# Decode attention block, forward and backward: the two batches staggered, so that forward heads of batch 1 run beside backward heads of batch 0

## The chip, the cores and the metric

One core of one Trainium2 chip. The metric is the device time of one execution in microseconds (us), the median of several. An execution with a profile takes as long as one without (the profiled execution of the kernel before took 1852.37 us; the others 1848 to 1858).

## The reference, cut to what matters

```python
B, Sq, D = (2, 1, 512);  H, Sk, Dh = (32, 8192, 128);  F = 1376
# forward (all bf16)
mod = silu(c) @ w_mod                       # 6 x 512 modulation values a batch
h   = layernorm(x) * (1 + ca) + sa
q   = h @ wq                                # one query a head
p   = softmax(q @ k_cache^T * Dh**-0.5)     # k_cache, v_cache: (2, 32, 8192, 128)
o   = p @ v_cache
x   = x + ga * (o @ wo)
h   = layernorm(x) * (1 + cb) + sb
x   = x + gb * ((silu(h @ w1) * (h @ w3)) @ w2)
# and the gradients of all inputs for a given grad_out:
# d_v_cache = p (outer) d_o,  d_k_cache = d_s (outer) q: the same 134 MB each as the caches
```

There are 64 heads (2 batches of 32). K and V of a head are 2.1 MB each, and so are its two gradients. In the forward pass a head needs K and V; in the backward pass it needs V again and writes two gradients. Between them lies a serial chain of small steps: output projection, FFN forward, FFN backward, back through the output projection. A batch's chain needs all 32 forward heads of that batch, and a batch's backward heads need that chain. Nothing ties the two batches to each other.

## The kernel before

The program gives each engine a list of instructions, and its author lays down their order by hand. The engines are named as in the profiles: PE (TensorE), DVE (VectorE), ACT (ScalarE), POOL (GpSimd), and SP (SyncE), which issues the loads here. The unit is a *slot*: 8 transposes of 128 x 128 blocks on PE, the copy of the 8 results out of PSUM (the memory that PE writes to), and what else is due. A head is 8 slots. This is the forward loop; the backward loop is built alike.

```python
NBIG = 10                                   # ten buffers of 16 KB a partition, for K, V, results and weights
def hb(i):
    return i % B, i // B                    # head i: the batches alternate
...
def mm_m(i, g):                             # 8 of the 64 blocks of a head: 16 matmuls
    ...
    for j in range(GRP):
        kk = g * GRP + j
        nc.tensor.matmul(m[:, 0:P + 1], V[i][:, kk, :], t[:, kk % QK, 0:P + 1], ...)
        nc.tensor.matmul(m[:, P + 1:P + 2], K[i][:, kk, :], E2[:, i, kk, 0:1], ...)
...
for t in range(NSLOT + MOFF + 1):           # forward: 64 heads x 8 slots
    i, g = divmod(t, NG)
    ...
    kts[(i, g)] = transposes(K[i], g, g in (2, 6))          # 8 transposes; copy by ACT, or by DVE in 2 of 8
    ...                                                     # 8 one-column matmuls with q: the scores
    scale_k(...)                                            # DVE: K times exp(scores), 4 pieces a head
    mm_m(mi, mg)                                            # 16 matmuls for an earlier head
    if mg == NG - 1:
        ...
        load(K, A_k_cache, mi + 4); load(V, A_v_cache, mi + 3)   # when a head is done
# [cut] the serial chain for both batches at once, in plain program order:
#       attn, x1, layernorm, w1, w3, silu, w2, transposes of w2, w1, w3 and wo, their products
for t in range(NSLOT + LAG + 2 * NQ + 4):   # backward: 64 heads x 8 slots
    kts[(n, g)] = transposes(V[order[n]], g, g in (2, 6))
    ...                                     # 8 one-column matmuls; DVE: outer products in 8 pieces a head
    half_store(...)                         # four stores of 1 MB a head, issued by GpSimd (POOL)
    ...                                     # one small "task" a slot: weight gradients and the like
```

Of the kernel before, what the change touches and what calls it, by code (L numbers as in the profile page):

```python
# [9 lines left out]
F32 = mybir.dt.float32  # L10
# [8 lines left out]
def kernel(  # L19
# [48 lines left out]
    NBIG = 10  # L68
# [4 lines left out]
    def hb(i):  # L73
        return i % B, i // B
# [7 lines left out]
    bigp = ctx.enter_context(tc.tile_pool(name="bigp", bufs=NBIG))  # L82
    ktp = ctx.enter_context(tc.tile_pool(name="ktp", bufs=5))
# [6 lines left out]
    def big():  # L90
        return bigp.tile([P, BIG], BF16, name="big", tag="big")

# [15 lines left out]
    E2 = cst.tile([P, NHD, KK, 2], BF16, name="E2")  # L108
# [31 lines left out]
    V = {}  # L140

    def load(store, src, i):
        b, h = hb(i)
        t = big()
        v = t[:, 0:KK * P].rearrange("p (k d) -> p k d", k=KK)
        qd.dma_start(v, src[b, h].rearrange("(p kk) d -> p kk d", p=P))
        store[i] = v
# [10 lines left out]
    load(K, A_k_cache, 0)  # L158
    load_wq(1)
    load(K, A_k_cache, 1)  # L160
    load_wq(2)
    load_wq(3)
    for a in range(2):
        qd.dma_start(wm_v[a][:, :, M1:MD], wm_d[:, 2 * a:2 * a + 2, M1:MD])
    load(V, A_v_cache, 0)
    load(K, A_k_cache, 2)
    load(V, A_v_cache, 1)
    load(K, A_k_cache, 3)
# [114 lines left out]
    evac_n = [0]  # L283

    def evac(dst, src):
        if evac_n[0] % 2 == 0:
            nc.scalar.copy(dst, src)
        else:
            nc.vector.tensor_copy(dst, src)
        evac_n[0] += 1  # L290

    S_ps = {}
    M_ps = {}
    ek = {}
    kts = {}
    M_t = {}
    MOFF = NG + LAG + 5
    NSLOT = NHD * NG

    def pair(ap, n):  # L300
        return ap.rearrange("p k (a b) -> p k a b", b=2)

    def transposes(src, g, dve):
        tp = tps.tile([P, GRP, P], BF16, name="tp", tag="tp")
        for j in range(GRP):
            nc.tensor.transpose(tp[:, j, :], src[:, g * GRP + j, :], identb[:])  # L306
        kt = ktp.tile([P, GRP, P], BF16, name="kt", tag="kt")
        if dve:
            nc.vector.tensor_copy(kt[:], tp[:])  # L309
        else:  # L310
            nc.scalar.copy(kt[:], tp[:])  # L311
        return kt

    def chain_rowmax(i):
        rm = hw.tile([P, 1], BF16, name="rm", tag="rm")
        nc.vector.tensor_reduce(rm[:], S_ps[i][:, 0:KK], AX.X, ALU.max)
        kts[("rm", i)] = rm

    def chain_b(i):
        s = S_ps[i]  # L320
        nc.tensor.matmul(s[:, P:2 * P], kts.pop(("rm", i))[:].to_broadcast((P, P)), nident[:],  # L321
                         start=True, stop=True)
        nm = hw.tile([P, 1], F32, name="nm", tag="nm")
        nc.vector.tensor_reduce(nm[:], s[:, P:2 * P], AX.X, ALU.min)  # L324
        kts[("nm", i)] = nm

    def chain_e(i):
        s = S_ps.pop(i)
        nc.scalar.activation(E2[:, i, :, :], s[:, 0:KK].unsqueeze(2).to_broadcast((P, KK, 2)), ACT.Exp,  # L329
                             bias=kts.pop(("nm", i))[:], scale=SCL, accum_out=rsum[:, i:i + 1])  # L330

    def scale_k(i, q):
        t = ekp.tile([P, QK, 130], BF16, name="ek", tag="ek")
        ks = slice(q * QK, (q + 1) * QK)
        nc.vector.tensor_tensor(pair(t[:, :, 0:P], QK), pair(K[i][:, ks, :], QK),  # L335
                                E2[:, i, ks, :].unsqueeze(2).to_broadcast((P, QK, P // 2, 2)), ALU.mult)
        nc.gpsimd.tensor_copy(t[:, :, P:P + 1], E2[:, i, ks, 0:1])  # L337
        ek[(i, q)] = t

    def mm_m(i, g):  # L340
# [3 lines left out]
        t = ek[(i, g // 2)]  # L344
        for j in range(GRP):
            kk = g * GRP + j
            nc.tensor.matmul(m[:, 0:P + 1], V[i][:, kk, :], t[:, kk % QK, 0:P + 1],  # L347
                             start=(kk == 0), stop=(kk == KK - 1), skip_group_check=True)
            nc.tensor.matmul(m[:, P + 1:P + 2], K[i][:, kk, :], E2[:, i, kk, 0:1],  # L349
                             start=False, stop=(kk == KK - 1), skip_group_check=True)  # L350
        if g == NG - 1:
            K.pop(i)

    def m_evac(i):
        m = M_ps.pop(i)
        nc.scalar.copy(M_all[:, i, :], m[:, 0:P])  # L356
        nc.vector.tensor_copy(OK[:, i, :], m[:, P:P + 2])  # L357

    KEEPV = 2
    extra = {}  # L360

    def at(slot, f):
        extra.setdefault(slot, []).append(f)

    for pc in range(1, NPC):
        at(2 * pc, lambda pc=pc: q_part(pc))
    at(NG, lambda: mod_part(2 * NC, MC))
# [3 lines left out]
    def load_wo():  # L371
        for a in range(2):
            t = big()
            v = t[:, 0:H // 2 * D].rearrange("p (h d) -> p h d", d=D)
            qd.dma_start(v, A_wo.rearrange("(h p) d -> p h d", p=P)[:, a * (H // 2):(a + 1) * (H // 2), :])
            wo_v.append(v)

    wn = {}
    nfull = F // P

    def load_ffn():
        for nm, ap in (("w1", B_w1), ("w3", B_w3)):
            t = big()
            wn[nm] = t[:, 0:NC * F].rearrange("p (k f) -> p k f", k=NC)
            qd.dma_start(wn[nm], ap.rearrange("(k p) f -> p k f", p=P))
        t = big()
        wn["w2"] = t[:, 0:FC * D].rearrange("p (k d) -> p k d", k=FC)
        qd.dma_start(wn["w2"][:, :nfull, :], B_w2[0:nfull * P].rearrange("(k p) d -> p k d", p=P))
        if FL != P:
            qd.dma_start(wn["w2"][:FL, nfull, :], B_w2[nfull * P:F])  # L390

    M_all = None
    Mt = None
    for t in range(NSLOT + MOFF + 1):
        i, g = divmod(t, NG)
        u = t - (NG + LAG + 2)
        if u >= 0 and u % NG == 0 and u // NG < NHD:
            chain_e(u // NG)
        if i < NHD:
            if g == 0:  # L400
                S_ps[i] = stps()
            kts[(i, g)] = transposes(K[i], g, g in (2, 6))
        for f in extra.pop(t, []):
            f()
        s = t - LAG
        if 0 <= s < NSLOT:
            si, sg = divmod(s, NG)
            b, h = hb(si)
            kt = kts.pop((si, sg))
            for j in range(GRP):  # L410
                cc = sg * GRP + j
                nc.tensor.matmul(S_ps[si][:, cc:cc + 1], kt[:, j, :], qT_bf[:, h, b:b + 1],  # L412
                                 start=True, stop=True)
        for off, f in ((0, chain_rowmax), (1, chain_b)):
            u = t - (NG + LAG + off)
            if u >= 0 and u % NG == 0 and u // NG < NHD:
                f(u // NG)
        u = t - (NG + LAG + 3)
        if u >= 0 and u % 2 == 0 and u // NG < NHD:
            scale_k(u // NG, (u % NG) // 2)  # L420
        u = t - MOFF
        if 0 <= u < NSLOT:
            mi, mg = divmod(u, NG)
            mm_m(mi, mg)
            if mg == NG - 1:
                if mi < NHD - KEEPV:
                    V.pop(mi)
                if mi + 4 < NHD:
                    load(K, A_k_cache, mi + 4)
                if mi + 3 < NHD:  # L430
                    load(V, A_v_cache, mi + 3)
                if mi == min(2, NHD - 5):
                    load_wo()
                if mi == NHD - 3:
                    load_ffn()
        if t == NG:
            load(V, A_v_cache, 2)
        u = t - MOFF - 1
        if u >= 0 and u % NG == NG - 1:
            if M_all is None:  # L440
                Mt = big()
                M_all = Mt[:, 0:NHD * P].rearrange("p (i d) -> p i d", d=P)
            m_evac(u // NG)

    woT = [big(), big()]
    woT_v = [t[:, 0:2 * HD].rearrange("p (k m) -> p k m", k=2) for t in woT]

    def tgroup(blocks, dsts):
        tp = tps.tile([P, GRP, P], BF16, name="tp", tag="tp")
        flat = tp[:].rearrange("p a b -> p (a b)")  # L450
        for o, n, src, rows in blocks:
            nc.tensor.transpose(flat[:n, o:o + rows], src, identb[:rows, :rows])
        for dst, (n, o, w, k) in dsts:
            s = flat[:n, o:o + w]
            if k > 1:
                s = s.rearrange("p (k m) -> p k m", k=k)
            evac(dst, s)

    def t_wo(a, h0):
        nh = min(4, H - h0)  # L460
        blocks = []
        for d2 in range(2):
            for hh in range(nh):
                h = h0 + hh
                src = wo_v[h // (H // 2)][:, h % (H // 2), (2 * a + d2) * P:(2 * a + d2 + 1) * P]
                blocks.append(((d2 * nh + hh) * P, P, src, P))
        tgroup(blocks, [(woT_v[a][:, :, h0 * P:(h0 + nh) * P], (P, 0, 2 * nh * P, 2))])

    tot = mtps()
    nc.tensor.matmul(tot[:, 0:NHD], onesf[:], rsum[:], start=True, stop=True)  # L470
    rtot = col("rtot", H)
    rtot_f = rtot[:].rearrange("p h b -> p (h b)")
    nc.vector.tensor_scalar(rtot_f, tot[:, 0:NHD], 0.5, None, ALU.mult)
# [531 lines left out]
```

## Time and profile before

| | |
|---|---|
| median of 5 runs | 1850.72 us (1848.03 to 1858.42) |
| busy share PE, DVE, ACT | 75%, 61%, 52% |
| moved by DMA | 709.57 MB, mean 383 GB/s |

The average shares say little, because three stages follow each other. First the page of the kernel before: busy share of PE, granted TensorE clock, DMA share in tenths (9 is 90% or more) and GB/s in 40 equal slices of 46 us.

```profile
span 1850.6 us, 58876 instructions
PE   5888999999999999978778777675655565566560
...
PEclk9999999999999999968555558577666556656665
DMA  9998999999999999549999999999999999999996
GB/s 391 411 358 323 385 382 392 389 372 378 356 366 369 364 371 365 220 161 357 413 411 416 416 420 421 399 415 420 421 419 418 418 418 418 420 423 423 418 417 282
DMA packets 79784, 709.57 MB, mean 383 GB/s; under 512 B 8160, under 2 KB 13644, under 8 KB 21932
```

Then the busy times cut into the stretches of the argument: stretch, its length, busy us (and instructions) of PE, weight load, DVE, ACT, POOL, the mean granted clock, the DMA share, GB/s. The cut at 461 us is where forward head 38 would start.

```profile
core 0: us, PE busy (x) PEld busy (x) DVE busy (x) ACT busy (x) POOL busy (x), PEclk, DMA share, GB/s
0.00:461.00 461.00, 414.35 (x9757) 408.37 (x9758) 245.07 (x364) 254.46 (x343) 83.44 (x153) 0.99 0.95 378
461.00:765.00 304.00, 282.96 (x6755) 279.13 (x6753) 171.08 (x239) 171.72 (x235) 57.35 (x105) 0.99 0.91 363
765.00:850.00 85.00, 69.89 (x1430) 65.77 (x1427) 46.73 (x107) 43.71 (x63) 7.16 (x10) 0.78 0.44 160
850.00:1800.00 950.00, 615.91 (x8582) 535.73 (x8579) 654.26 (x692) 481.80 (x602) 150.26 (x278) 0.62 1.01 417
1800.00:1850.60 50.60, 3.77 (x80) 3.29 (x78) 15.72 (x17) 3.89 (x4) 5.84 (x11) 0.57 0.70 294
```

And the waits of PE between 200 and 750 us of the kernel before: engine, line, what it waited for, us in total, times, longest.

```profile
PE m_ps L347 <- issue: 9.5, 12, 1.7
PE m_ps L349 <- issue: 7.9, 11, 1.1
PE tp L306 <- issue: 7.9, 10, 1.1
PE s_ps L412 <- issue: 4.5, 7, 0.8
```

Reading them together:

- Forward, to 765 us: PE is busy over 90% of the time at full clock, and it waits for no other engine and for no load: its entries are all "issue" (time in which it waited for nothing that the profile shows), 30 us of 550. DMA stays at 363 to 378 GB/s. So this stage is taken to be PE-bound, at about 11.5 us a head, where the 4.19 MB of a head need 10.0 us at 418 GB/s.
- The chain, 765 to 850 us: neither is full; 160 GB/s.
- Backward, from 850 us: 417 GB/s with a DMA share of 1.01, PE at a clock of 0.62 and still idle a third of the time. This stage is DMA-bound. Loads and stores share this ceiling although two engines issue them; the Trainium skill ("Trainium Kernel Development and Optimization", Key Constraints) says that the queues of SP, ACT and POOL run on the same 16 DMA engines and interleave, which the one share of 1.01 for both agrees with.

A measure used from here on: the *lost DMA time* of a stretch is its length less its bytes divided by 418 GB/s, the rate of the backward stage. The bytes of a kernel over 418 GB/s plus all its lost DMA time is its span. Before: 1697.5 + 153.1 us.

### The profile page before, as it was taken

The page shows a single profiled execution, that of the slowest core. Times are in us where ns is not written, and L with a number is a line of the kernel's source. Part 1 is how long each engine was busy: PE and PEld are TensorE (multiplying, and loading weights), DVE is VectorE, ACT ScalarE, POOL GpSimd, SP SyncE. Part 2 cuts the span into 40 slices and gives each one's busy share as a digit, 9 for nine tenths or more (in the row PEclk, how much of TensorE's full clock was granted, in tenths as well). Part 3 has the DMA queues.
Part 4 walks back from the last instruction along what each step waited for, and adds up shares of the span by engine and source line. Part 5 has one row for each costly group of instructions (what it writes and reads, how often), then busy time and mean ns, then how long its engine had stood idle before and what let it go on. Part 6 is the DMA issues. An engine that isn't in the chain of part 4 may idle for free. (4 is left out here: it accounts for less than half of the span.)

```text
span 1850.6 us, 58876 instructions
## 1 busy us (share of the span) xinstructions
PE 1386.9 (75%) x26588; PEld 1292.3 (70%) x26588; DVE 1132.9 (61%) x1415; ACT 955.6 (52%) x1244; POOL 304.1 (16%) x557
## 2 busy tenths in 40 slices
PE   5888999999999999978778777675655565566560
PEld 5888999999899999876556566474555555555550
DVE  2455656565555555548565647577876667777682
ACT  3545656556555555348546566474444344444440
POOL 0111212122122211102121111111111111111111
PEclk9999999999999999968555558577666556656665
DMA  9998999999999999549999999999999999999996
GB/s 391 411 358 323 385 382 392 389 372 378 356 366 369 364 371 365 220 161 357 413 411 416 416 420 421 399 415 420 421 419 418 418 418 418 420 423 423 418 417 282
DMA packets 79784, 709.57 MB, mean 383 GB/s; under 512 B 8160, under 2 KB 13644, under 8 KB 21932
## 3 DMA queue, kind: packets, MB, share of 16 engines
q1 hardware_dynamic: 38304, 421.57, 56.7%
q0 software_dynamic: 41216, 284.22, 36.9%
q8 instruction: 208, 3.41, 0.7%
q14 instruction: 44, 0.36, 0.1%
q10 hardware_dynamic: 12, 0.01, 0.0%
HBM read 421.57 MB, written 284.20 MB: 381 GB/s over the span
## 5 line engine op out<-in xcount | busy, mean ns | idle before, releaser
L311 ACT COPY kt<-tp 128x1024 bf16<-128x1024 bf16 x768 | 776.2, 1014 | 675.6 <-PE tp L306 665.8
L306 PE MATMUL tp<-identb,big 128*128 128x128 bf16 x8192 | 796.8, 255 | 28.0 <-issue 15.6
L306 PEld LDWEIGHTS <-big 128*128 128x128 bf16 x8192 | 599.9, 114 | 125.3 <-issue 118.0
L347 PE MATMUL m_ps<-ek,big 128*128 128x129 bf16 x4096 | 411.6, 218 | 11.3 <-issue 10.8
L349 PE MATMUL m_ps<-E,big 128*128 128x1 bf16 x4096 | 383.3, 165 | 11.1 <-issue 10.9
L958 PE MATMUL s_ps<-DO_bf,kt 128*128 128x1 bf16 x4096 | 195.7, 169 | 259.2 <-DVE kt L309 258.7
L958 PEld LDWEIGHTS <-kt 128*128 128x128 bf16 x4096 | 191.5, 110 | 278.9 <-DVE kt L309 277.8
L895 DVE TENSOR_TENSOR big<-QD,E 128x2048 bf16<-128x2048 bf16 x256 | 311.7, 1218 | 116.8 <-DMA out_dram<-big 67.9
L895 DVE TENSOR_TENSOR big<-QD,ds 128x2048 bf16<-128x2048 bf16 x256 | 312.0, 1220 | 91.7 <-PE tp L306 60.6
L309 DVE COPY kt<-tp 128x1024 bf16<-128x1024 bf16 x256 | 176.3, 689 | 302.9 <-PE tp L306 260.6
L347 PEld LDWEIGHTS <-big 128*128 128x128 bf16 x4096 | 346.5, 96 | 14.8 <-issue 14.4
L349 PEld LDWEIGHTS <-big 128*128 128x128 bf16 x4096 | 344.0, 96 | 11.5 <-issue 11.1
L335 DVE TENSOR_TENSOR ek<-big,E 128x2048 bf16<-128x2048 bf16 x256 | 306.7, 1219 | 3.0 <-ACT E L329 2.2
L903 POOL DMA_DIRECT2D out_dram<-big x256 | 136.3, 532 | 822.8 <-DVE big L895 356.2
L337 POOL COPY ek<-E 128x16 bf16<-128x16 bf16 x256 | 143.9, 564 | 626.2 <-ACT E L329 274.2
L412 PE MATMUL s_ps<-qT_bf,kt 128*128 128x1 bf16 x4096 | 178.2, 164 | 12.5 <-issue 9.5
L412 PEld LDWEIGHTS <-kt 128*128 128x128 bf16 x4096 | 158.7, 97 | 16.2 <-issue 12.7
L710 ACT CAST stg<-m_ps 128x512 bf16<-128x512 f32 (+2 forms) x123 | 71.9, 593 | 109.2 <-DMA out_dram<-stg 77.0
L709 PE MATMUL m_ps<-big 2*128 2x512 bf16 (+2 forms) x123 | 71.3, 580 | 38.2 <-ACT stg L710 38.1
L324 DVE TENSOR_REDUCE nm<-s_ps 128x1 f32<-128x128 f32 x64 | 18.7, 292 | 57.9 <-PE s_ps L321 57.9
L357 DVE COPY OK<-m_ps 128x2 f32<-128x2 f32 x64 | 10.2, 159 | 59.2 <-ACT big L356 59.2
L890 ACT CAST QD<-m_ps 128x256 bf16<-128x256 f32 x64 | 24.7, 386 | 11.1 <-PE m_ps L887 11.1
(198 smaller groups left out, 483.8 us busy)
## 6 DMA issues: line engine op xcount, KB each, us to landing
out_dram<-big POOLq DMA_DIRECT2D x256, 1024.0 KB, 28.8
big<-in_A_v_cache_dram SPq DMA_DIRECT2D x126, 2048.0 KB, 13.7
big<-in_A_k_cache_dram SPq DMA_DIRECT2D x64, 2048.0 KB, 9.8
out_dram<-stg POOLq DMA_DIRECT2D x22, 512.0 KB, 19.8
big<-in_A_wq_dram SPq DMA_DIRECT2D x8, 512.0 KB, 14.4
big<-in_A_wo_dram SPq DMA_DIRECT2D x2, 2048.0 KB, 17.3
big<-in_A_wq_dram SPq DMA_DIRECT2D x2, 2048.0 KB, 15.3
big<-in_w_mod_dram SPq DMA_DIRECT2D x2, 1536.0 KB
```

What stands on the lines that cost most here:

```text
L306: nc.tensor.transpose(tp[:, j, :], src[:, g * GRP + j, :], identb[:])
L309: nc.vector.tensor_copy(kt[:], tp[:])
L311: nc.scalar.copy(kt[:], tp[:])
L335: nc.vector.tensor_tensor(pair(t[:, :, 0:P], QK), pair(K[i][:, ks, :], QK), E2[:, i, ks, :].unsqueeze(2).to_broadcast((P, QK, P // 2, 2)), ...
L337: nc.gpsimd.tensor_copy(t[:, :, P:P + 1], E2[:, i, ks, 0:1])
L347: nc.tensor.matmul(m[:, 0:P + 1], V[i][:, kk, :], t[:, kk % QK, 0:P + 1], start=(kk == 0), stop=(kk == KK - 1), skip_group_check=True)
L349: nc.tensor.matmul(m[:, P + 1:P + 2], K[i][:, kk, :], E2[:, i, kk, 0:1], start=False, stop=(kk == KK - 1), skip_group_check=True)
L412: nc.tensor.matmul(S_ps[si][:, cc:cc + 1], kt[:, j, :], qT_bf[:, h, b:b + 1], start=True, stop=True)
L710: nc.scalar.copy(st["t"][:lw, o:o + rw], ps[:lw, 0:rw])
L895: nc.vector.tensor_tensor(pair(dst[:, ks, :], QK), QD[n][:, which, :].rearrange("p (a b) -> p a b", b=2).unsqueeze(1).to_broadcast((P, QK, ...
L903: sq_.dma_start(dst_dram[b, h].rearrange("(p kk) d -> p kk d", p=P)[:, ks, :], t[:, ks, :])
L958: nc.tensor.matmul(DP[sn][:, cc:cc + 1], kt[:, j, :], DO_bf[:, h, b:b + 1], start=True, stop=True)
```

## The change

Intent: put the PE-bound forward work beside the DMA-bound backward work. The heads are ordered batch by batch. All forward heads of batch 0 run; the chain of batch 0 ("chain 0") is cut into 57 small steps, laid two to a slot between the forward slots of batch 1's first heads; then forward heads of batch 1 and backward heads of batch 0 alternate ("pairs"); the chain of batch 1 ("chain 1") is laid under the last backward heads of batch 0; then come batch 1's backward heads with the weight gradients, as before.

It costs something. The chain's transposes of w1, w3 and wo are done once for each batch; the products with w2's transpose become dot products on DVE. The FFN weights are dropped after chain 0 and loaded again for chain 1. V tiles are no longer kept over the turn from forward to backward. The buffers are 5 big ones and 11 of half the size, and a load takes whichever kind is free.

```diff
-    NBIG = 10
+    NBIG = 5
+    NHALF = 11
...
     def hb(i):
-        return i % B, i // B
+        return i // H, i % H
...
+    sA = [NG * i for i in range(H)]                 # start slots of the forward heads
+    CS0 = end_a(sA[H - 1]) + 1                      # chain 0 starts
+    TC = CS0 + (length(ch[0]) + 1) // 2 + 1         # and ends
...
+    while len(sA) < NHD:
+        if s >= TC and len(sC) < H and (not sC or sC[-1] < s - NG):
+            sC.append(s)                            # a backward head of batch 0
+        else:
+            sA.append(s)                            # a forward head of batch 1
+        s += NG
...
+    CS1 = end_a(sA[NHD - 1]) + 1
+    lay(dh[1], lay(dh[0], FS0) + 1)                 # the dot products with w2
+    lay_half(ch[0], CS0)
+    t1 = lay_half(ch[1], CS1)
+    s = max(s, t1 + 4)
+    sC += [s + NG * n for n in range(H)]            # backward heads of batch 1
...
+    for a in range(2):
+        want(FS0 - 3 + a, "big", lambda a=a: load_ffn(a))
+        want(CS0 - 3 + a, "big", lambda a=a: load_wo(a))
+        want(CS1 + a, "big", lambda a=a: load_ffn(a))      # the second load of the FFN weights
...
+    at(TC, PL_TASK, ffn_done)                       # drops the FFN weights
+    at(sC[0] - 6, PL_FREE, start_keep)              # from here 2 half buffers are kept for results
```

(The comments are added here. Cut: the bookkeeping of slots and loads, the chain rewritten as steps, the forward and backward parts under new names.) By these rules 38 forward heads come before the first pair, there are 26 pairs, and chain 1 lies under six backward heads.

## The prediction

> **What bounds it now.** Three stages, read from the engine-busy table cut into stretches.
> (1) Forward, 0 to about 765 us. PE is busy 96% of 200-400 us at clock 1.00, and waits there for nothing but its own issue (list of waits). The exp of heads 0 and 35 start at 41.1 and 443.9 us: 11.5 us a head. The loads need only 4.19 MB a head, 10.0 us at 418 GB/s, and DMA runs at 370-384 GB/s. PE-bound.
> (2) The serial chain (output projection, FFN forward and backward), about 765-850: DMA falls to 3 GB/s at 780-800; some 57 us of DMA time are lost.
> (3) Backward, 850 to the end: 414-421 GB/s, DMA share 1.01: DMA-bound, 6.3 MB and about 15 us a head; PE clock 0.61-0.70.
> 709.6 MB at 418 GB/s would take 1697 us; the other 153 us are forward 79, chain 57, end 15.
>
> **What the change does.** Batch by batch: 38 forward heads, the chain of batch 0 laid between the forward slots of heads 32-37, then 26 pairs of one forward head of batch 1 and one backward head of batch 0, then the chain of batch 1 under six backward heads, then 32 backward heads with the weight gradients. PE-bound forward work is set beside DMA-bound backward work; about half of the big buffers become half-size.
>
> **Costed.**
> - Bytes: no V tiles kept over the turn (+4.2 MB), FFN weights twice (+4.2 MB): 718 MB, 1717 us at 418 GB/s (+20).
> - Forward-only stage: head 38 would start at about 461 us by the measured 1.44 us a slot. Chain 0 now sits on the bounding engine: about 28 groups of 8 transposes and 8 matmuls, 0.66 us each from the trace's spacings (56 and 26 ns), plus some 260 one-column matmuls: 25 us, with waits about 40; dot products on DVE about 5. So the pairs start at about 505 us, with about 181 MB loaded (433 us of DMA): 73 us lost.
> - Pairs: 10.5 MB, 25.1 us of DMA. PE needs 11.5 + 5.3 = 16.8 us at full clock, DVE about 17.6, ACT about 14: DMA should bind. The doubt is the clock. The Trainium skill ("TensorE: Matmul & The Clock Gate", Part 1) says that the array runs at half clock until a window of about 3.4 us was busy, and falls back after an idle one; this trace agrees: at 1300-1358 us it alternates between 0.50 and 1.00, going cold after idle gaps of about 5 us. All at half clock, a pair would need about 30 us. I expect oscillation, 0.3 us a pair lost: 8 us.
> - Chain 1 is hidden under backward heads: 0-5 us. End: about 15 us, as now.
> Sum: 1717 + 73 + 8 + 15 = about 1812 us. The 57 us gap goes and 26 forward heads stop being PE-bound; chain 0's PE time and 20 us of bytes are paid.
>
> Predicted: **1812 us**, 80% range 1775 to 1850. Faster by over 2%: 0.52; within 2%: 0.43; slower by over 2%: 0.05.
>
> **What would show each step.** No slice of the DMA row near zero in the middle; first backward-V transposes at 490-520 us; before that 345-375 GB/s; after it at least 405 nearly to the end; PE clock 0.7 to 1.0 in the pairs; 717-719 MB; forward slots of heads 32-37 about 2.3 us.
>
> **What would make it wrong.** Slower: PE cold in the pairs, so that a pair takes 27-30 us (+50 to +120); PE waiting for K or V because a load sits behind a store for its half buffer; GpSimd's in-order queue holding forward copies behind store issues; chain 0 waiting 1-2 us at each of its 57 steps. Faster: chain 0 hides between forward slots, or more is prefetched.

(Read again from the trace: the idle gaps of PE at 1300 to 1358 us that go before half clock are 6.2 to 7.4 us long, not about 5, and the clock falls 2.5 to 3.1 us after they begin.)

## The result, and the profile after

The changed kernel took 1828.36 us (median of 9; 1825.49 to 1834.32), the kernel before 1852.03 us on the same chip (median of 16). The ratio is 0.9871, 95% interval 0.9852 to 0.989: 1.3% faster, within the 2% that count as the same.

The page of the changed kernel, the same rows:

```profile
span 1824.9 us, 60769 instructions
PE   6888999999887777777878777757976867768363
...
PEclk9999999997987888788787778858655555767665
DMA  9998999996599999999999999989999999999997
GB/s 384 422 413 336 383 396 391 378 364 239 202 404 404 419 422 422 416 412 423 419 422 418 424 416 415 415 350 370 419 406 410 411 424 419 418 422 399 425 399 308
DMA packets 98993, 718.11 MB, mean 394 GB/s; under 512 B 10112, under 2 KB 16972, under 8 KB 26284
```

The dip at 765 to 850 us is gone from the middle. But there is a new one in slices 10 and 11 (about 410 to 500 us, 239 and 202 GB/s) and a shallow one in slices 27 and 28 (350 and 370). The stretches of the changed kernel are forward heads 0-31; chain 0; pairs; chain 1; the rest of the backward heads; the end:

```profile
core 0: us, PE busy (x) PEld busy (x) DVE busy (x) ACT busy (x) POOL busy (x), PEclk, DMA share, GB/s
0.00:410.00 410.00, 366.58 (x8638) 359.97 (x8639) 231.88 (x375) 227.21 (x308) 101.94 (x168) 1.00 0.97 385
410.00:520.00 110.00, 97.51 (x2203) 94.92 (x2201) 72.07 (x165) 42.21 (x59) 15.87 (x31) 0.89 0.66 247
520.00:1150.00 630.00, 490.65 (x9689) 474.68 (x9688) 423.16 (x500) 324.24 (x450) 107.80 (x225) 0.81 1.01 418
1150.00:1270.00 120.00, 79.61 (x1647) 74.97 (x1645) 71.72 (x139) 67.26 (x90) 14.60 (x25) 0.77 0.93 373
1270.00:1750.00 480.00, 344.48 (x4448) 272.76 (x4446) 304.21 (x340) 288.89 (x443) 82.44 (x150) 0.60 1.01 415
1750.00:1824.90 74.90, 35.09 (x598) 33.04 (x596) 58.35 (x61) 29.32 (x40) 12.22 (x23) 0.64 0.84 342
```

Worked out from finer slices of the same view, at 418 GB/s:

| lost DMA time, us | before | after |
|---|---|---|
| first forward heads | 43.7 (to 461 us, heads 0-37) | 32.4 (to 410 us, heads 0-31) |
| chain 0, with forward heads 32-37 | in the chain below | 45.0 |
| the other 26 forward heads | 40.2 | 0.0 (the pairs) |
| chain of both / chain 1 | 52.4 | 12.9 |
| backward | 1.7 | 3.4 |
| end | 15.1 | 13.2 |
| sum | 153.1 | 106.9 |
| bytes / 418 GB/s | 1697.5 (709.57 MB) | 1718.0 (718.11 MB) |
| span | 1850.6 | 1824.9 |

So 40 us came from the forward heads that are now in pairs, and 40 from the chain (52.4 less 12.9). Against them stand 34 us for chain 0, which now lies in the PE-bound stage (32.4 + 45.0 against 43.7), and 20 us for 8.5 MB more. What is left is 26 us.

Chain 0 can be timed by the exp instruction of the forward heads, one a head. In the kernel before, heads 32 and 37:

```profile
410.50 0.37 ACT L329 ACTIVATE E<-s_ps,nm 128x128 bf16<-128x128 f32 x1
...
466.05 0.37 ACT L329 ACTIVATE E<-s_ps,nm 128x128 bf16<-128x128 f32 x1
```

In the changed kernel, heads 32 and 37:

```profile
408.63 0.37 ACT L425 ACTIVATE e<-s_ps,nm 128x128 bf16<-128x128 f32 x1
...
506.46 0.37 ACT L425 ACTIVATE e<-s_ps,nm 128x128 bf16<-128x128 f32 x1
```

The columns are start, duration, engine, line, operation. Both kernels reach head 32 within 2 us of each other. The next five heads take 55.6 us before and 97.8 us with chain 0 between their slots: 42 us more. In the pairs the 25 exps from 533.0 to 1135.6 us are 25.1 us apart, the DMA time of 10.5 MB. There PE is at a clock of 0.81 and idle 22% of the time: it no longer binds.

Where the 42 us go can be read from PE's instructions between these two exps, each given the time until the next one starts, less idle time. The chain's own instructions take 28.7 us. The forward slots' instructions take 59.6 us instead of 52.9, which goes with a clock at half for 23.9 us. PE is idle for 9.6 us instead of 2.7; in the list of waits 7.3 us of this are waits for DVE. That is 28.7 + 6.7 + 6.9 us.

The longest waits of PE in chain 1 of the changed kernel, 1150 to 1270 us (L740 is the first product with w1 or w3; L387 the transposes of K and V):

```profile
PE s_ps L740 <- DMA big<-in_B_w_dram: 11.8, 1, 11.8
PE tp L387 <- DMA big<-in_A_v_cache_dram: 6.7, 2, 5.9
PE s_ps L678 <- DVE O_bf L670: 5.2, 1, 5.2
```

### The profile page after: what moved, and what is told of

It reads as the page before. It is cut to its first block, busy times and chain, and to the rows that moved or that the text cites. A ratio compares the mean times of both kernels' runs of the same rounds, so it can differ in the third digit from the quotient of the medians. Undisturbed runs are those within 1.5% of the kernel's fastest.

```text
span 1824.9 us, 60769 instructions
## 1 busy us (share of the span) xinstructions
PE 1413.9 (77%) x27206; PEld 1310.3 (72%) x27206; DVE 1161.4 (64%) x1574; ACT 979.1 (54%) x1387; POOL 334.9 (18%) x621
## 2 busy tenths in 40 slices
DMA packets 98993, 718.11 MB, mean 394 GB/s; under 512 B 10112, under 2 KB 16972, under 8 KB 26284
## 4 chain that ended last, share of the span: by engine, by line
PE 33%; DMA 33%; issue 22%; DVE 6%; POOL 2%; ACT 2%; POOLq 0%; DVEq 0%; SPq 0%; ACTq 0%
DMA out_dram<-half 23%; PE m_ps L448 13%; PE tp L387 12%; DVE half L986 4%; PE s_ps L407 3%; DMA big<-in_A_v_cache_dram 2%; DMA half<-in_A_k_cache_dram 2%; DMA big<-in_B_w_dram 2%; POOL out_dram L991 2%; DMA out_dram<-stg 1%; ACT kt L392 1%; DMA big<-in_w_mod_dram 1%; DVE ek L433 1%; DVE kt L390 1%; PE tp L634 1%
## 5 line engine op out<-in xcount | busy, mean ns | idle before, releaser
L387 PE MATMUL tp<-identb,half 128*128 128x128 bf16 x5056 | 442.4, 238 | 21.3 <-issue 12.7
L450 PE MATMUL m_ps<-e,half 128*128 128x1 bf16 x4096 | 407.4, 170 | 6.1 <-issue 5.9
L986 DVE TENSOR_TENSOR half<-DOr,e 128x2048 bf16<-128x2048 bf16 x256 | 311.8, 1218 | 123.7 <-DMA out_dram<-half 116.7
L986 DVE TENSOR_TENSOR half<-Qr,ds 128x2048 bf16<-128x2048 bf16 x256 | 309.9, 1220 | 97.6 <-DMA out_dram<-half 96.7
L387 PEld LDWEIGHTS <-half 128*128 128x128 bf16 x5056 | 335.9, 107 | 44.7 <-issue 37.3
L450 PEld LDWEIGHTS <-half 128*128 128x128 bf16 x4096 | 353.9, 97 | 5.8 <-issue 5.8
L387 PE MATMUL tp<-identb,big 128*128 128x128 bf16 x3136 | 326.9, 268 | 13.1 <-DMA big<-in_A_v_cache_dram 13.1
L387 PEld LDWEIGHTS <-big 128*128 128x128 bf16 x3136 | 246.8, 120 | 107.3 <-issue 92.7
L433 DVE TENSOR_TENSOR ek<-half,e 128x2048 bf16<-128x2048 bf16 x256 | 307.7, 1219 | 2.5 <-ACT e L425 2.2
L448 PE MATMUL m_ps<-ek,half 128*128 128x129 bf16 x2240 | 249.7, 229 | 62.4 <-DVE ek L433 60.6
L448 PEld LDWEIGHTS <-half 128*128 128x128 bf16 x2240 | 212.6, 107 | 64.1 <-issue 63.9
L448 PE MATMUL m_ps<-ek,big 128*128 128x129 bf16 x1856 | 186.3, 218 | 3.4 <-issue 3.4
L448 PEld LDWEIGHTS <-big 128*128 128x128 bf16 x1856 | 156.7, 96 | 5.7 <-issue 5.7
```

What stands on the lines that cost most here:

```text
L387: nc.tensor.transpose(tp[:, j, :], block(j), identb[:])
L433: nc.vector.tensor_tensor(pair(t[:, :, 0:P]), pair(K[(i, hf)][:, o:o + QK, :]), E2[i][:, ks, :].unsqueeze(2).to_broadcast((P, QK, P // 2, ...
L448: nc.tensor.matmul(m[:, 0:P + 1], vb_(V[i], kk), t[:, kk % QK, 0:P + 1], start=(kk == 0), stop=(kk == KK - 1), skip_group_check=True)
L450: nc.tensor.matmul(m[:, P + 1:P + 2], kb_(K, i, kk), E2[i][:, kk, 0:1], start=False, stop=(kk == KK - 1), skip_group_check=True)
L986: nc.vector.tensor_tensor(pair(t[:, o:o + QK, :]), QD[(n, which)][:].rearrange("p (a b) -> p a b", b=2).unsqueeze(1).to_broadcast((P, QK, ...
```

## The experiments

All were run beside the kernel before on the same chip, five rounds each, and all are correct. They form three groups, each on a chip of its own: e0 to e3, e4 to e7, and e8 with e9. The changed kernel itself was run again as a reference in the first two. Times are medians; ratios are to the kernel before.

| run | edit | us | ratio |
|---|---|---|---|
| e0, e4 | the changed kernel again | 1829.1, 1829.0 | 0.9862, 0.9851 |
| e1 | pairs start at head 50 instead of 38 | 1847.5 | 0.9965 |
| e2 | FFN weights kept, no second load | 1823.6 | 0.9840 |
| e3 | one-column products of the chains widened | 1826.5 | 0.9847 |
| e5 | second FFN load asked for earlier | 1825.4 | 0.9834 |
| e6 | transposes of chain 0 doubled | 1838.4 | 0.9909 |
| e7 | transposes of chain 1 doubled | 1828.6 | 0.9846 |
| e8 | half of the FFN weights kept | 1817.6 | 0.9782 |
| e9 | e2, with 1 half buffer reserved instead of 2 | 1826.2 | 0.9833 |

The interval of a ratio is plus or minus 0.002 to 0.003, about 4 to 5.5 us. Differences between variants below that, such as those of e3, e5 and e7 from the changed kernel, are not clear of noise by it.

### e0 and e4: the changed kernel again

> The changed kernel again, as the reference of this group on the same chip: about 1828 us (ratio to before about 0.987).

> The changed kernel once more, as the reference of this group on its chip: ratio to before about 0.987.

1829.1 and 1829.0 us. The trace repeats: lost DMA time of 45.0 and 44.5 us in chain 0, -1.5 us twice in the pairs, 13.5 and 12.9 in chain 1. So these three sums repeat within 2 us. The stretch before them does not: up to 410 us, where the changed kernel and all variants do the same, the loss is 32 to 38 us in their eleven traces. A difference of a few us between two whole traces means little.

### e1: is it the pairing, or only the hidden chain?

```diff
-        if s >= TC and len(sC) < H and (not sC or sC[-1] < s - NG):
+        if s >= max(TC, NG * 50) and len(sC) < H and (not sC or sC[-1] < s - NG):
```

(By the author's account all 64 forward heads before the first backward head would not fit, as the ring of kept exps would be too long for the memory, and head 50 is near the limit. No run shows this.)

> Only the start of the pairs is moved: from forward head 38 to forward head 50 (14 pairs in place of 26); chain 0 stays between the slots of heads 32-37. Theory (pairing turns PE-bound forward heads into DMA-bound pairs): 12 more forward heads run PE-bound at about 11.2 us while their loads need 10.0 us, so about 14 us slower than the changed kernel (1838 to 1846), and the slices from 500 to about 640 us show 360-395 GB/s instead of 420. Rival (all the gain is the hidden chain, pairing by itself gives nothing): within 4 us of the changed kernel.

18 us slower than e0, a little more than expected, and it takes away three quarters of the gain (ratio 0.9965 against 0.9862). The stretch 520 to 720 us of e1, which had pairs before, then the same stretch of the changed kernel:

```profile
520.00:720.00 200.00, 174.56 (x4014) 171.03 (x4011) 122.83 (x159) 112.03 (x155) 49.02 (x81) 0.96 0.93 372
```

```profile
520.00:720.00 200.00, 156.00 (x3096) 150.76 (x3095) 133.49 (x159) 102.90 (x144) 36.47 (x72) 0.82 1.01 418
```

372 instead of 418 GB/s over 200 us is 22 us of lost DMA time, against 18 us measured in the whole. Pairing gives about 1.5 us a pair (18 / 12). The rival falls. Whether the half-size buffers would gain anything without the staggering was not tested; in the kernel before PE waited for no load from 200 to 750 us.

### e6 and e7: is chain 0 PE work, and is chain 1?

```diff
-            for j, src in enumerate(blocks):
-                nc.tensor.transpose(tp[:r, j, :], src, identb[:])
+            for _ in range(2 if b == 0 else 1):         # e7: b == 1
+                for j, src in enumerate(blocks):
+                    nc.tensor.transpose(tp[:r, j, :], src, identb[:])
```

> Every transpose of the w1, w3 and wo groups in chain 0 is done twice (same result): 216 more transposes, 12 us of PE work at full clock by 56 ns each. Theory (chain 0 costs what its PE work is, because PE is the bounding engine there): pairs start 11 to 17 us later and the kernel is 11 to 17 us slower than the changed kernel. Rival (chain 0 is made of waits between engines, PE has room): less than 5 us slower.

> The same doubling in chain 1, which lies under DMA-bound backward heads. Theory (there PE work is free as long as the store and load queues are full): at most 3 us slower than the changed kernel. Rival (chain 1's lost DMA time is PE work too, and at half clock): 8 to 15 us slower, loss at 1200-1270 us grows by that.

Doubled in chain 0 the kernel takes 9.4 us more than e4; doubled in chain 1 it takes 0.4 us less, which is nothing. Heads 32 and 37 of e6, by their exps:

```profile
414.56 0.37 ACT L425 ACTIVATE e<-s_ps,nm 128x128 bf16<-128x128 f32 x1
...
520.65 0.37 ACT L425 ACTIVATE e<-s_ps,nm 128x128 bf16<-128x128 f32 x1
```

That is 106.1 us, 8.3 more than the 97.8 of the changed kernel. Of 12.1 us of added PE work (216 transposes of 56 ns) 8 to 11 us reach the end of the program (8.3 in the trace, 9.4 by the medians, 10.8 by the ratios), at or a little under the low end of the 11 to 17 expected: most PE work in chain 0 is paid for. Part of the rest fell into waits that were there anyway: PE's waits for DVE in this part are 4.8 us in e6, and 7.3 in the changed kernel. The same instructions cost nothing measurable where DMA binds. So chain 0 is mostly PE work in the wrong place, and chain 1's loss does not grow with PE work. One thing dulls e7: from 1225 to 1275 us its clock stood at 1.00 where the changed kernel had 0.88, so part of the added work was done at a faster clock.

### e3: does the clock matter in chain 0?

The clock record of the changed kernel falls to half for 23.9 us in chain 0, in pieces of 13.7 and 10.2 us. They begin at 420.4 us, among the 128 one-column matmuls of the output projection (416.9 to 425.2), and at 437.5 us, among the 88 of w1 and w3 (435.4 to 438.3). PE shows no wait of over 2 us there.

```diff
-                                 O_bf[:, b, h:h + 1], start=(h == 0), stop=(h == H - 1))
+                                 O_bf[:, b, h:h + 1].to_broadcast((P, 64)), start=(h == 0), stop=(h == H - 1))
...   # likewise 23 columns for w1 and w3, 64 for w2; the results are taken from the first column
```

> Same instructions, but the one-column products of the chains (output projection, FFN up and down: 260 matmuls a chain) move 64 or 23 equal columns instead of 1. Theory (the clock gate looks at what streams through the array: bursts of one-column matmuls let the clock fall to half for about 24 us in chain 0, at about 421-448 us): clock 1.00 through chain 0, pairs start about 10 us earlier, about 10 us faster than the changed kernel. Rival (the clock falls because PE waits in the chain, or the half clock costs nothing there): clock record as before, time within 4 us, or slower by the wider columns (260 x 0.03 us = 8 us a chain).

The stretch 415 to 460 us of e3, then of the changed kernel:

```profile
415.00:460.00 45.00, 38.04 (x868) 37.27 (x869) 22.23 (x66) 16.04 (x23) 5.54 (x10) 0.89 0.64 241
```

```profile
415.00:460.00 45.00, 40.93 (x870) 39.86 (x868) 24.08 (x71) 15.63 (x22) 4.18 (x9) 0.73 0.55 203
```

The half-clock time in chain 0 falls to 10.2 us; in the other ten traces of the changed kernel and its variants it is 17.1 to 23.9 us. So the widening seems to have kept the clock up for part of it, but the program gains only 2.7 us on e0, inside the spread, and heads 32 to 37 take 98.9 us (e0: 98.1). The expected 10 us did not come. The wider columns cost something themselves: the spacing of the output projection's matmuls rose from 26 to 31 ns and that of w2's from 27 to 53, some 2 us in all. So e3 alone does not say what the half clock costs. The other traces do: of the nine whose chain 0 is unchanged, the three with 17.1 us at half clock take 95.7 to 96.0 us for heads 32 to 37, and the six with 20.5 to 23.9 us take 97.7 to 98.1. That is 2 us for up to 6.8 us of half clock, so about 7 us of chain 0's 42 (an estimate from these traces), as much as the 6.7 us by which the forward slots' instructions took longer. The half clock is not the main part of chain 0. That narrow matmuls let the clock fall is supported by one run, not settled.

### e5, e2, e9, e8: what the second load of the FFN weights costs

e5 asks for the load earlier:

```diff
-        want(CS1 + a, "big", lambda a=a: load_ffn(a))
+        want(CS1 - 24 + a, "big", lambda a=a: load_ffn(a))
```

> The second load of the FFN weights is asked for 24 slots earlier (same bytes as the changed kernel). Theory (chain 1's 13 us of lost DMA time are the 11.8 us wait for that load, and PE has room for the rest of the chain): the wait for the FFN weights disappears, the loss at 1200-1250 us falls to 5 us or less, the kernel is 5 to 10 us faster than the changed kernel. Rival (chain 1's own steps of 2 us and more make the loss, the wait is only the first of them): loss stays above 10 us, time within 3 us.

3.6 us faster than e4, less than expected and within the intervals. The wait for the weights is gone, but these stand in the same place, in the waits of PE in e5 from 1150 to 1270 us:

```profile
PE tp L387 <- DMA half<-in_A_v_cache_dram: 8.4, 1, 8.4
PE tp L387 <- DMA half<-in_A_k_cache_dram: 6.6, 1, 6.6
```

That the weights took buffers which V and K then lacked fits this, and is argued rather than shown. The loss moved forward, from 1200-1250 to 1150-1250 us, and is 10.9 us from 1150 to 1270 instead of e4's 13.0.

e2 loads the weights once:

```diff
-        want(CS1 + a, "big", lambda a=a: load_ffn(a))
-    at(TC, PL_TASK, ffn_done)
```

> The FFN weights stay in their two big buffers from chain 0 to chain 1 and are not loaded a second time; in the pairs V then has only half buffers. Theory A (chain 1's 13 us of lost DMA time are mostly the 11.8 us wait for the second FFN load, and 4.2 MB cost 10 us at 418 GB/s): 713.9 MB, no wait for the FFN weights in chain 1, 16 to 24 us faster than the changed kernel (1804-1812). Theory B (chain 1's loss is its own chain of steps; only the bytes go): about 10 us faster. Theory C (the half buffers are too few without two big ones): the pairs fall below 405 GB/s and the kernel is slower.

5.5 us faster than e0 (ratios 0.9840 and 0.9862, whose intervals overlap), much less than theory A and less than B. Theory C's mechanism shows, but smaller than it said: the pairs fall to 414 GB/s, not below 405, and the kernel is not slower. Pairs and chain 1 of e2:

```profile
520.00:1150.00 630.00, 474.34 (x9564) 456.28 (x9562) 418.41 (x495) 318.32 (x447) 137.07 (x220) 0.81 1.01 414
1150.00:1270.00 120.00, 94.03 (x1920) 88.97 (x1919) 84.81 (x159) 76.21 (x101) 19.51 (x33) 0.77 0.99 395
```

By stretches: 4.2 MB less is 10 us, chain 1 loses 6.6 instead of 12.9 us, but the pairs lose 6.0 instead of 0.0 us, and the change from chain 0 to the pairs 5 us more (chain 0's stretch 49.7). That sums to about -6 us. e9 is e2 with `KEEP = 1`:

> As e2 (all FFN weights kept), but only one half buffer instead of two is held back from the loads for the results of the backward heads. If the loads of K are late in e2 because too few half buffers are given to loads, the waits of PE for K in the pairs (80 us in e2) fall by more than half and the time falls to about 1816 (ratio 0.979); if loads are late because their buffer still waits for its store, nothing gained or slower than e2's ratio of 0.984.

1826.2 us, no gain (ratio 0.9833 against 0.9840). These are lines of the waits between 520 and 1150 us. First PE in e2 and DVE in the changed kernel (L986 writes the gradients into half buffers):

```profile
PE tp L387 <- DMA half<-in_A_k_cache_dram: 85.9, 18, 8.7
```

```profile
DVE half L986 <- DMA out_dram<-half: 140.1, 47, 7.1
```

Then PE and DVE in e9 (L984 is the same statement as L986):

```profile
PE s_ps L407 <- DVE kt L390: 112.2, 23, 6.4
```

```profile
DVE half L984 <- DMA out_dram<-half: 169.3, 25, 8.5
```

In e2 DVE has no entry of this kind at all, and PE waits for K. With one buffer fewer reserved, PE's wait for K falls to 7.7 us, as the first half of the expectation said, but DVE waits for the stores that must free its result buffers, and PE for DVE. The second half's outcome holds: time does not move. Here the wait went to whichever side had too few buffers.

e8 keeps one of the two big buffers of FFN weights and loads the other again, asked for 8 slots earlier:

```diff
-        want(CS1 + a, "big", lambda a=a: load_ffn(a))
+    want(CS1 - 8, "big", lambda: load_ffn(1))
...
-        wn.clear()
-        release("big", 2)
+        wn.pop("w3")
+        wn.pop(("w2", 1))
+        release("big", 1)
```

> Of the FFN weights w1 and the first half of w2 stay in their big buffer; w3 and the second half are dropped after chain 0 and loaded again, asked for 8 slots earlier than in the changed kernel. If e2's loss in the pairs came from V and K sharing too few half buffers, one big buffer for V gives most of it back: pairs lose under 3 us (e2: about 12), 716.0 MB (5 us less than the changed kernel), chain 1 loses about 5: 1817 to 1822, ratio to before about 0.980, faster than e2 and e5. If buffers are not the reason, it lands between the changed kernel and e2 (about 1826).

1817.6 us, ratio 0.9782 (0.9762 to 0.9802): 2.2% faster than the kernel before (the record's class is "unclear", since the interval reaches past 0.98), and its interval lies below those of the changed kernel (0.985 to 0.987), e2 and e5. The expectation was met: the pairs lose 2.4 us (under 3), chain 1 loses 5.9 (about 5). Pairs and chain 1 of e8:

```profile
520.00:1150.00 630.00, 482.92 (x9596) 466.16 (x9594) 423.66 (x499) 321.74 (x448) 131.03 (x224) 0.80 1.01 416
1150.00:1270.00 120.00, 93.24 (x1891) 88.66 (x1888) 80.63 (x155) 73.93 (x98) 13.54 (x28) 0.76 0.98 398
```

The pairs keep 416 GB/s (changed kernel 418, e2 414), chain 1 has 398 instead of 373, and 716.05 MB are moved. This version beats both kernels. It was not compared with the changed kernel in the same rounds.

## Why the prediction was right or wrong

The prediction was 1812 us (1775 to 1850), and the kernel took 1828. The range held. The class with the larger chance (faster by over 2%, 0.52) was not what came; the other (within 2%, 0.43) did: 1.3% faster. The mechanism was right but for chain 1, and the sum can be compared term by term, since it was made of bytes and lost DMA time:

| term | predicted | measured | |
|---|---|---|---|
| bytes at 418 GB/s | 1717 | 1718.0 | right |
| forward heads and chain 0 | 73 | 77.4 | right to 4 us |
| pairs | 8 | 0.0 | better |
| chain 1 | 0-5 | 12.9 | too small |
| backward heads after it | 0 | 3.4 | |
| end | 15 | 13.2 | right |
| sum | 1812 | 1824.9 (the profiled span) | |

- *PE-bound forward, DMA-bound backward.* Right. e1 shows that pairing by itself is worth 1.5 us a pair; e6 and e7 show that the same PE instructions cost 9 us in the one place and nothing in the other.
- *Chain 0 costs 45 us where it lies.* Right in size: heads 32-37 took 42 us longer. Its make-up was given as 25 us of PE work and 15 us of waits. Measured, it is 28.7 us of the chain's own PE work, 6.9 us more idle time, and 6.7 us by which the forward slots' instructions took longer while the clock was at half. The doubling supports PE work as the main part. The clock's fall was not foreseen; that the waits were put too high made up for it, which is luck. "Forward slots about 2.3 us": 97.8 us for 40 slots is 2.4.
- *The pairs run at the DMA ceiling.* Right: 418 GB/s and 25.1 us a pair. "I expect oscillation, 0.3 us a pair lost" was too careful: the clock does oscillate (mean 0.81), and no DMA time is lost, since PE is busy only 78% of the time at that clock.
- *"Chain 1 is hidden under backward heads: 0-5 us".* This is the term that was mis-sized: it lost 12.9 us. That the whole error of the sum is also 13 is chance: the pairs' -8 cancels +4, +3 and the rest. The prediction counted the second FFN load as bytes only, and not as a wait. PE stood 11.8 us before it. e5 shows that this is not the whole story: taking that wait away brought 3.6 us by the medians, not clear of noise, and PE then waits 15.0 us for V and K in the same place. Without any second load chain 1 still loses 6.6 us (e2) or 10.5 us (e9), and with half of it 5.9 us (e8). e2, e9 and e8 show how a buffer given to one side is missed by another. How the 12.9 us divide between the late load, the buffers and the chain's own short steps is not settled; doubled PE work did not add to them (e7).
- *What would make it wrong* named loads behind stores for their half buffers. In the changed kernel the loads of K do wait on stores (532 us in total on SP's queue from 520 to 1150 us), yet the pairs stay at the ceiling; only with fewer free buffers (e2, e9) did the pairs lose 6 us and more. The "1-2 us at each of its 57 steps" did not come: PE's waits for DVE in chain 0 are 7.3 us in all.

## What to carry to other kernels

If one stage is bound by an engine and another by DMA, laying them side by side can gain what the first leaves of DMA time, as long as the engines have room (here 40 us, with PE busy 78% of the pairs), and this can be worked out beforehand: length of each stage less its bytes over the ceiling rate. But a serial chain laid under the engine-bound stage was not hidden here (42 us longer for its five heads), and under the DMA-bound one it nearly was (12.9 us lost). Chain 0 had no such place, since the first backward heads need it. And when DMA is near its ceiling, count buffers as well as bytes: here a weight buffer kept or given up moved as much time as the load that it saved.

## What the Trainium skill lacked or had wrong

- "TensorE: Matmul & The Clock Gate", Part 1, has the array at half clock by default and at full clock after a busy window of about 3.4 us. The traces agree on the window: half-clock pieces of 3.4, 10.2 and 13.7 us are 1, 3 and 4 of them. In all twelve traces every such piece is a whole number of them, but for those that the end cuts off. What it lacks is whether one-column matmuls count as busy in that window: in chain 0 of the changed kernel PE was busy 40.9 of 45 us (415 to 460) and the mean clock was 0.73, with bursts of one-column matmuls in it; with 64 or 23 columns instead of one the clock was 0.89. One run; it changed the time by under 3 us.
- "Runtime: NRT & Kernel Launch", Instruction fetch mechanics, has instructions fetched in blocks of 16 KiB (256 instructions) and the cost "mostly hidden". The size agrees: the queue of kind "instruction" of the changed kernel moved 213 blocks of 16,384 bytes for 54,412 PE instructions. In the first part of the PE-bound stage the cost seems not to be hidden. From 60 to 185 us of the changed kernel the trace's DMA records have 20 such blocks, 6.1 us apart, and PE's starts have 18 gaps of over 0.5 us, 20.2 us in all, each of which opens 0.9 to 1.7 us after a block's transfer began; from 200 to 330 us it was 24 blocks, 5.4 us apart, and 2 gaps, 2.2 us. In the kernel before it was 16 gaps with 20.4 us and 7 with 5.3. The "issue" entries among PE's waits fit this: a forward head took 12.6 us in the first stretch, and often 10.5 in the second, with the same instructions and the clock at 1.00 in nearly all of both. That the fetch makes the gaps is read from this coincidence alone; why they come with nearly every block at first and rarely later, no run here shows.
- No page that was read says how much a wait moves when a fixed set of buffers is divided anew. Here, with the FFN weights kept (e2) PE waited 86 us for K and DVE not at all for stores; with one half buffer more for the loads (e9) it was 7.7 us for K and 169 us of DVE for stores, and the time was the same.
